# Token routing in a fused scan, gated-MLP and expert kernel: one-hots in bf16, running sums by matmul, gate factors after the counts, addresses read when wanted

## The chip, the cores and the metric

The kernel runs on one core of a Trainium2 chip. The metric is the device time in microseconds of one execution. Five engines appear in the rows: PE (TensorE; PEld is its weight load), DVE (VectorE), ACT (ScalarE), POOL (GpSimd) and SP (SyncE, which here only issues DMAs). Most DMAs are issued from SP's queue, the indirect ones from POOL's.

## What is computed

Cut to what matters here, the reference is three layers in a row over 3072 tokens of 384 features:

```python
x = attn(q, k, v, alpha)                    # gated linear recurrence, 4 x 8 heads
x = moe(x, w_gate, w_val, w_out, rms_g)     # RMS norm, silu(x Wg) * (x Wv), then W_out
logits = x @ r_gate                         # 8 experts
e_idx = argmax(logits, 1)
probs = softmax(logits)
gate = probs[arange(N), e_idx]
eom = sigmoid(x @ r_ogate)
for e in range(8):
    rows = e_idx == e
    out[rows] = gate[rows, None] * eom[rows, e, None] * (relu(x[rows] @ w1[e]) @ w2[e])
```

The routing of the last layer is what the change touches: which expert each token goes to, the token's gate factor, and its place in that expert's list.

## The kernel before, in words

The tokens go through the first two layers in eight groups of 384 (`NG` groups of `GT` = 3 tiles of 128). After a group's last matmul of the second layer, `m_evac` (L689) copies its three tiles out of PSUM into a tile R of 400 columns: 384 features, 8 logits, 8 output-gate logits.

`route_a` (L709) then works on 128 x 3 x 8 numbers at a time, nearly all on DVE: the maximum, the differences, a one-hot of the maximum as float32 (ties broken by `rev8`), a bf16 copy of it (`ohb`), running sums of the three tiles' one-hots in bf16 (`ohc`), the exponentials by way of tanh on ACT, their sum (`se`) and the output gate (`og`). `route_b` (L744) counts with matmuls into a PSUM tile `ps_r` (L748 to L752): a strictly triangular matrix gives a token's rank in its tile, an all-ones matrix on `ohc` adds the tiles in front. DVE makes the gate factor (L755 to L757), the rank (L760 to L763), the row number `pos` (L766) and the new counts `cnt` (L767). Three indirect DMAs from POOL's queue (L769) scatter the rows of R into a `bucket` in DRAM, one region per expert. Groups 0 to 6 are routed while the next group's matmuls run; the last group's routing has no next group behind it.

The experts follow, in order of size. Expert slot 0 is split into two units u = 0 and u = 1 of 256 rows; then one unit per slot. The first unit's rows, weights and first matmuls are prepared from the counts of the first seven groups, so they do not wait for the last group. A unit runs through eight blocks j: `e_h(u, j)` (L1175) is nine matmuls (L650) into `ps_h`, with an eviction by ACT (L1184) and DVE (L1185); `e_o(u, j)` (L1189) is six matmuls (L1211, or L1205 for the slots that are computed transposed). `pop_o` issues `e_o` some blocks behind `e_h`.

Around the last group the program reads: e_h(0,0), the last MLP matmuls, `m_evac`, `route_a(7)` (L1337), e_h(0,1), then in the loop e_h(0,2), e_o(0,0), `route_b(7)` (L1509), `pick_rest` (L1042; it ranks the experts by count and writes the address table `adr`, L1056), the loads of slot 1's weights (L1083, L1098), the rows of unit 1 (L1130, which reads the bucket and so waits for the last scatter), more weights, and the rows of unit 2 (L1136). `addresses(p)` (L1023) reads a slot's three addresses (row region, w1 row, w2 row) from `adr` into SP registers, all three at once (L1025), before the first DMA that uses one. Slot 1's weights are split into a high and a low part by ACT and DVE (L1090, L1091, L1109, L1110) during unit 1.

What sets the order: a scheduler lays out each engine's queue at build time from its own estimate of readiness. `keep_in_program_order` (also called `pin` and, when `strict[0]` is set, `seq`) ties an instruction behind the one written just before it on its engine; everything else may be moved. In the last group `strict` is off until `route_b(7)`, so the scheduler may put e_o(0,1) and e_o(0,2) in front of `ps_r` on PE.

Of the kernel before, what the change touches and what calls it, by code (L numbers as in the profile page):

```python
# [55 lines left out]
def gla_glu_moe_kernel(  # L56
# [120 lines left out]
    def f(x):  # L177
        return x.bitcast(F32)
# [530 lines left out]
    def route_a(g):  # L709
        R = rows[g]  # L710
        L, O = R[:, :, DM:DM + E], R[:, :, DM + E:WO]
        bc = [P, GT, E]
        mx = small("mx", [P, GT, 1])
        nc.vector.tensor_reduce(out=mx, in_=L, op=ALU.max, axis=AX.X)
        ex = small("ex", bc)
        nc.vector.tensor_tensor(out=ex, in0=L, in1=mx.to_broadcast(bc), op=ALU.subtract)
        oh = small("oh", bc)
        nc.vector.tensor_scalar(out=oh, in0=ex, scalar1=0.0, scalar2=None, op0=ALU.is_ge)

        nc.scalar.activation(ex, ex, AF.Tanh, scale=0.5)  # L720
        er_ = small("er_", bc)
        nc.vector.tensor_scalar(out=er_, in0=ex, scalar1=-1.0, scalar2=1.0, op0=ALU.mult, op1=ALU.add)
        nc.vector.reciprocal(out=er_, in_=er_)
        nc.vector.scalar_tensor_tensor(out=ex, in0=ex, scalar=1.0, in1=er_, op0=ALU.add, op1=ALU.mult)
        nc.vector.tensor_tensor(out=oh, in0=oh, in1=rev8.to_broadcast(bc), op=ALU.mult)
        m8 = small("m8", [P, GT, 1])
        nc.vector.tensor_reduce(out=m8, in_=oh, op=ALU.max, axis=AX.X)
        nc.vector.tensor_tensor(out=oh, in0=oh, in1=m8.to_broadcast(bc), op=ALU.is_equal)
        ohb = small("ohb", [P, GT, E], BF16)
        nc.vector.tensor_copy(ohb, oh)  # L730
        ohc = small("ohc", [P, GT, E], BF16)
        nc.vector.tensor_copy(ohc[:, 0, :], oh[:, 0, :])
        nc.vector.tensor_tensor(out=ohc[:, 1, :], in0=oh[:, 0, :], in1=oh[:, 1, :], op=ALU.add)
        nc.vector.tensor_tensor(out=ohc[:, 2, :], in0=ohc[:, 1, :], in1=oh[:, 2, :], op=ALU.add)
        sg = small("sg", bc)
        nc.vector.tensor_tensor(out=sg, in0=oh, in1=O, op=ALU.mult)
        og = small("og", [P, GT, 1])
        nc.vector.tensor_reduce(out=og, in_=sg, op=ALU.add, axis=AX.X)
        nc.scalar.activation(og, og, AF.Tanh, scale=0.5)
        se = small("se", [P, GT, 1])  # L740
        nc.vector.tensor_reduce(out=se, in_=ex, op=ALU.add, axis=AX.X)
        rt[g] = (oh, ohb, ohc, m8, og, se)

    def route_b(g):  # L744
        oh, ohb, ohc, m8, og, se = rt.pop(g)
        R = rows[g]
        ps = psR[0].tile([P, GT + 1, E], F32, tag=psR[1], name="ps_r")
        seq(nc.tensor.matmul(ps[:, 0:1, :], lhsT=tri_b, rhs=ohb[:, 0:1, :], start=True, stop=True))  # L748
        for i in range(1, GT):
            seq(nc.tensor.matmul(ps[:, i, :], lhsT=tri_b, rhs=ohb[:, i, :], start=True, stop=False))  # L750
            seq(nc.tensor.matmul(ps[:, i, :], lhsT=ones_b, rhs=ohc[:, i - 1, :], start=False, stop=True))
        seq(nc.tensor.matmul(ps[:, GT, :], lhsT=ones_b, rhs=ohc[:, GT - 1, :], start=True, stop=True))  # L752
        bc = [P, GT, E]

        nc.vector.tensor_scalar(out=se, in0=se, scalar1=1e-9, scalar2=2.0, op0=ALU.add, op1=ALU.mult)  # L755
        nc.vector.reciprocal(out=se, in_=se)
        nc.vector.scalar_tensor_tensor(out=R[:, :, DM:DM + 1], in0=og, scalar=1.0, in1=se, op0=ALU.add, op1=ALU.mult)  # L757
        nc.vector.tensor_copy(R[:, :, DM + 1:DM + 2], tokid[:, g * GT:g * GT + GT, :])
        rk = small("rk", bc)
        nc.vector.tensor_tensor(out=rk, in0=ps[:, 0:GT, :], in1=cnt.to_broadcast(bc), op=ALU.add)  # L760
        nc.vector.tensor_tensor(out=rk, in0=rk, in1=oh, op=ALU.mult)
        pf = small("pf", [P, GT, 1])
        nc.vector.tensor_reduce(out=pf, in_=rk, op=ALU.add, axis=AX.X)  # L763
        nc.vector.tensor_scalar(out=m8, in0=m8, scalar1=-float(REG), scalar2=float(E * REG), op0=ALU.mult, op1=ALU.add)
        pos = small("pos", [P, GT, 1], I32)
        nc.vector.tensor_tensor(out=pos, in0=pf, in1=m8, op=ALU.add)  # L766
        nc.vector.tensor_tensor(out=cnt[:, 0, :], in0=cnt[:, 0, :], in1=ps[:, GT, :], op=ALU.add)  # L767
        for i in range(GT):
            nc.gpsimd.indirect_dma_start(out=bucket_of[g * GT + i], out_offset=OFF(ap=pos[:, i, 0:1], axis=0),  # L769
                                         in_=R[:, i, 0:RW], in_offset=None)  # L770
# [247 lines left out]
    places = {}  # L1018
# [60 lines left out]
    def load_w1(p, i):  # L1079
        n = F2 // 4  # L1080
        s = slice(i * n, i * n + n)
        st = staging("st1", [P, KD, n])
        ins = nc.sync.dma_start(st, w1.rearrange("e k n -> (e k) n")[bass.ds(places[p][1], DM), s]  # L1083
                                .rearrange("(p kc) n -> p kc n" if p else "(kc p) n -> p kc n", p=P))
        if p > 1:
            pin(ins)

        def go():
            w1h, w1l = we[p][0:2]
            for ins in (nc.scalar.activation(w1h[:, :, s], st, AF.Copy),  # L1090
                        nc.vector.tensor_tensor(out=w1l[:, :, s], in0=st, in1=f(w1h[:, :, s]), op=ALU.subtract)):  # L1091
# [33 lines left out]
    def load_rows(u, er):  # L1125
        p, s0, r, n = parts[u]
        rows_ = bucket[bass.ds(places[p][0], CMAX), :]
        ix = act.tile([P, 4, 1], I32, tag="ix", name="ix", bufs=4)
        if u < 2:
            nc.sync.dma_start(er[:, 0:n, :], rows_[s0:s0 + P * n, :].rearrange("(p b) w -> p b w", b=n))  # L1130
            erow[u] = (er, ix, er[:, :, DM:DM + 1], er[:, :, RW - 1:RW])
            return
# [42 lines left out]
    def e_h(u, j):  # L1175
# [4 lines left out]
        else:  # L1180
# [3 lines left out]
        nc.scalar.activation(hh[:, 0, :], ps, AF.Relu)  # L1184
        nc.vector.scalar_tensor_tensor(out=hh[:, 1, :], in0=ps, scalar=0.0, in1=f(hh[:, 0, :]),  # L1185
                                       op0=ALU.max, op1=ALU.subtract)
        h2[u, j] = hh

    def e_o(u, j, tiles=None):  # L1189
# [18 lines left out]
        for i in range(n) if tiles is None else tiles:  # L1208
            sl = slice(i * r, i * r + r)
            for m, (a_, b_) in enumerate(((0, 2), (0, 3), (1, 2))):  # L1210
                ins = nc.tensor.matmul(ob2[u][i][0:r], lhsT=hh[:, a_, sl], rhs=we[p][b_][:, j, :],  # L1211
                                       start=(j == 0 and m == 0), stop=(j == KF2 - 1 and m == 2))
                if tiles is not None:
                    tc.keep_in_program_order(ins)
# [264 lines left out]
    def pop_o():  # L1479
        u, j = lag.pop(0)  # L1480
        e_o(u, j)
# [11 lines left out]
    for u in range(U):  # L1493
        for j in range(KF2):
# [4 lines left out]
            e_h(u, j)  # L1499
# [95 lines left out]
```

## Time and profile before

| | |
|---|---|
| median of 3 runs | 820.66 us (820.44 to 821.23) |
| the profiled execution | 820.86 us |
| its span, first to last instruction | 819.0 us |
| mean granted TensorE clock | 0.997 |
| PE / DVE / ACT / POOL busy | 98% / 69% / 40% / 11% of the span |
| DMA moved | 106.85 MB, mean 130 GB/s |

A row of the timeline gives start and length in us, the engine, the line of the kernel, the operation, the tile written and the tiles read, and, in square brackets, the idle time of that engine just before it with what ended it. A row of the waits gives who waited for whom, the total, the number of times and the longest, all in us.

### The profile page before, as it was taken

The page shows a single profiled execution, that of the slowest core. Times are in us where ns is not written, and L with a number is a line of the kernel's source. Part 1 is how long each engine was busy: PE and PEld are TensorE (multiplying, and loading weights), DVE is VectorE, ACT ScalarE, POOL GpSimd, SP SyncE. Part 2 cuts the span into 40 slices and gives each one's busy share as a digit, 9 for nine tenths or more (in the row PEclk, how much of TensorE's full clock was granted, in tenths as well). Part 3 has the DMA queues.
Part 4 walks back from the last instruction along what each step waited for, and adds up shares of the span by engine and source line. Part 5 has one row for each costly group of instructions (what it writes and reads, how often), then busy time and mean ns, then how long its engine had stood idle before and what let it go on. Part 6 is the DMA issues. An engine that isn't in the chain of part 4 may idle for free.

```text
span 819.0 us, 15897 instructions
## 1 busy us (share of the span) xinstructions
PE 802.6 (98%) x5967; PEld 771.7 (94%) x5967; DVE 561.4 (69%) x1234; ACT 326.5 (40%) x694; POOL 91.3 (11%) x175
## 2 busy tenths in 40 slices
PE   7999999999999999999999999999999999999996
PEld 5899999999999999999999999999988999999996
DVE  7998999498677876767767662345358667677641
ACT  1756554333333333332433332225226455554441
POOL 3001000000300020010020011010021002211121
PEclk9999999999999999999999999999999999999998
DMA  9955575753543453344444221005047686688710
GB/s 200 215 142 153 160 163 167 214 142 95 146 111 92 113 130 76 83 112 96 102 115 102 47 46 44 20 21 183 1 142 209 169 223 186 214 245 251 204 54 28
DMA packets 195454, 106.85 MB, mean 130 GB/s; under 512 B 125868, under 2 KB 190122, under 8 KB 195376
## 3 DMA queue, kind: packets, MB, share of 16 engines
q1 hardware_dynamic: 190912, 96.35, 46.2%
q0 software_dynamic: 4464, 9.48, 3.5%
q8 instruction: 47, 0.77, 0.4%
q14 instruction: 31, 0.25, 0.1%
HBM read 80.88 MB, written 25.18 MB: 129 GB/s over the span
## 4 chain that ended last, share of the span: by engine, by line
PE 93%; issue 2%; DVE 2%; POOL 1%; ACT 1%; DMA 0%; POOLq 0%; DVEq 0%
PE ps_o L684 19%; PE ps_v L650 19%; PE ps_g L650 19%; PE ps_h L650 12%; PE ps_b L1205 8%; PE ps_s L430 3%; PE ps_b L1211 3%; PE ps_y L468 3%; PE ps_y L464 2%; PE ps_st L489 1%; PE pc L615 1%; PE ps_k L450 1%; PE ps_n L283 1%; DMA er<-bucket 0%; PE pt L607 0%
## 5 line engine op out<-in xcount | busy, mean ns | idle before, releaser
L664 ACT ACTIVATE hh<-tt 128x384 fp32r<-128x384 f32 x96 | 50.3, 524 | 143.2 <-DVE tt L661 133.2
L661 DVE TENSOR_TENSOR tt<-tt,ps_v 128x384 f32<-128x384 f32 x96 | 52.7, 549 | 77.8 <-PE ps_v L650 65.7
L642 ACT ACTIVATE tt<-ps_g 128x384 f32<-128x384 f32 x96 | 47.0, 490 | 86.1 <-PE ps_g L650 80.3
L670 DVE TENSOR_TENSOR hl<-tt,hh 128x384 fp32r<-128x384 f32 x96 | 52.9, 551 | 24.6 <-ACT hh L664 23.0
L1185 DVE SCALAR_TENSOR_TENSOR h<-ps_h,h 128x256 fp32r<-128x256 f32 (+6 forms) x72 | 38.1, 531 | 45.2 <-ACT h L1184 42.5
L684 PE MATMUL ps_o<-wol,hh 128*128 128x400 f32 x192 | 66.3, 346 | 0.0
L684 PE MATMUL ps_o<-woh,hh 128*128 128x400 f32 x192 | 65.2, 348 | 0.0
L1184 ACT ACTIVATE h<-ps_h 128x256 fp32r<-128x256 f32 (+6 forms) x72 | 33.5, 468 | 77.4 <-PE ps_h L650 76.5
L684 PE MATMUL ps_o<-woh,hl 128*128 128x400 f32 x192 | 63.7, 344 | 0.0
L650 PE MATMUL ps_h<-x,w1b 128*128 128x456 f32 (+3 forms) x288 | 57.2, 341 | 0.3 <-DVE h L1185 0.3
L650 PEld LDWEIGHTS ps_h<-x,w1b 128*128 128x128 f32 x288 | 50.6, 188 | 1.9 <-DVE h L1185 0.6
L650 PE MATMUL ps_h<-x,w1a 128*128 128x256 f32 (+3 forms) x288 | 52.2, 325 | 0.0
L650 PEld LDWEIGHTS ps_h<-x,w1a 128*128 128x128 f32 x288 | 47.3, 188 | 0.9 <-ACT x L1165 0.3
L650 PE MATMUL ps_g<-xh,wgh 128*128 128x384 f32 x192 | 46.1, 348 | 0.0
L440 DVE TENSOR_TENSOR P<-ps_s,mask 128x512 f32<-128x512 f32 x46 | 30.1, 685 | 23.0 <-PE ps_s L430 22.8
L650 PE MATMUL ps_v<-xh,wvh 128*128 128x384 f32 x192 | 45.8, 346 | 0.0
L650 PE MATMUL ps_v<-xl,wvh 128*128 128x384 f32 x192 | 44.1, 337 | 0.0
L1205 PE MATMUL ps_b<-h,w2b 128*128 128x456 f32 (+2 forms) x216 | 43.5, 343 | 0.5 <-issue 0.5
L650 PE MATMUL ps_g<-xh,wgl 128*128 128x384 f32 x192 | 44.0, 336 | 0.0
L650 PE MATMUL ps_g<-xl,wgh 128*128 128x384 f32 x192 | 43.8, 337 | 0.0
L650 PE MATMUL ps_v<-xh,wvl 128*128 128x384 f32 x192 | 43.8, 336 | 0.0
L1205 PEld LDWEIGHTS ps_b<-h,w2b 128*128 128x128 f32 x216 | 37.9, 188 | 2.2 <-issue 0.9
(312 smaller groups left out, 1880.3 us busy)
## 6 DMA issues: line engine op xcount, KB each, us to landing
st<-in_moe_w_dram SPq DMA_DIRECT2D x46, 384.0 KB
bucket<-zero SPq DMA_DIRECT2D x8, 772.0 KB
stg<-in_moe_w_gate_dram SPq DMA_DIRECT2D x12, 384.0 KB
stg<-in_moe_w_val_dram SPq DMA_DIRECT2D x12, 384.0 KB
stg<-in_moe_w_out_dram SPq DMA_DIRECT2D x12, 384.0 KB
v<-in_v_dram SPq DMA_DIRECT2D x23, 192.0 KB
more<-in_moe_w_dram SPq DMA_DIRECT2D x9, 384.0 KB
er<-in_moe_w_dram SPq DMA_DIRECT2D x9, 384.0 KB
```

Of the source, the lines that this page charges most:

```text
L430: seq(nc.tensor.matmul(ps[hh][:, p, :], lhsT=kT[r, p, :], rhs=qT[r, p, :], start=True, stop=True))
L440: pace(f'Ph{t}', nc.vector.tensor_tensor(out=Ph, in0=ps[hh], in1=mb, op=ALU.mult))
L468: seq(nc.tensor.matmul(ps[u, h * D:h * D + D], lhsT=Pt[h % 2][:, h // 2, u], rhs=vt[t][:, h, :], start=first, stop=True, skip_group_check= ...
L642: nc.scalar.activation(tt, ps, AF.Silu)
L650: seq(nc.tensor.matmul(ps, lhsT=a_[:, kc, :], rhs=b_[:, kc, :], start=(n == 0), stop=(n == 3 * KD - 1)))
L661: nc.vector.tensor_tensor(out=tt, in0=tt, in1=ps, op=ALU.mult)
L664: nc.scalar.activation(hh, tt, AF.Copy)
L670: nc.vector.tensor_tensor(out=hl, in0=tt, in1=f(hh), op=ALU.subtract)
L684: seq(nc.tensor.matmul(obank[s][i], lhsT=a_[:, sl], rhs=weight(b_, j), start=(j == j0 and n == 0), stop=(j == j1 - 1 and n == 2)))
L1184: nc.scalar.activation(hh[:, 0, :], ps, AF.Relu)
L1185: nc.vector.scalar_tensor_tensor(out=hh[:, 1, :], in0=ps, scalar=0.0, in1=f(hh[:, 0, :]), op0=ALU.max, op1=ALU.subtract)
L1205: nc.tensor.matmul(ob2[u][k_][:, 0:r * n], lhsT=we[p][b_][:, j, k_ * P:k_ * P + P], rhs=hh[:, a_, :], start=(j == 0 and m == 0), stop=(j = ...
```

## The change

The routing of a group becomes one function that hands out eight steps, so that the last group's steps can be put in another order than the other groups'. The float32 one-hot, its bf16 copy and the three instructions of `ohc` become one comparison that writes bf16; the comparison with zero and the product with `rev8` become one instruction. The sums over the tiles in front are made by matmuls of the all-ones matrix with each tile's one-hot: nine matmuls a group in place of six. In the last group the product `sg`, the scaling of `m8` and the copy of the token numbers go to POOL, the DVE steps are pinned in the written order, and the gate factor comes after `pos`. The eviction of e_h(0,2) is written after `route_b(7)` with its DVE half pinned there, and e_o(0,1) is pinned where it is written, behind e_h(0,3). Addresses are read one at a time, when the first DMA that wants one is written; the DMAs of slot 1's weights and of unit 1's rows are now pinned.

```diff
-    def route_a(g):
+    def routing(g):
         R = rows[g]
+        end = g == NG - 1
         L, O = R[:, :, DM:DM + E], R[:, :, DM + E:WO]
...
+        side_ = nc.gpsimd if end else nc.vector
+        def order(ins):
+            if end:
+                tc.keep_in_program_order(ins)
+        def pick():
...
+            nc.vector.tensor_reduce(out=mx, in_=L, op=ALU.max, axis=AX.X)
+            order(nc.vector.tensor_tensor(out=ex, in0=L, in1=mx.to_broadcast(bc), op=ALU.subtract))
+            order(nc.vector.scalar_tensor_tensor(out=oh, in0=ex, scalar=0.0, in1=rev8.to_broadcast(bc),
+                                                 op0=ALU.is_ge, op1=ALU.mult))
+            nc.scalar.activation(ex, ex, AF.Tanh, scale=0.5)
+            order(nc.vector.tensor_reduce(out=m8, in_=oh, op=ALU.max, axis=AX.X))
+            order(nc.vector.tensor_tensor(out=ohb, in0=oh, in1=m8.to_broadcast(bc), op=ALU.is_equal))
+            ins = side_.tensor_tensor(out=sg, in0=ohb, in1=O, op=ALU.mult)
+            if not end:
+                order(ins)
+                order(nc.vector.tensor_reduce(out=og, in_=sg, op=ALU.add, axis=AX.X))
+                nc.scalar.activation(og, og, AF.Tanh, scale=0.5)
+            ins = side_.tensor_scalar(out=m8, in0=m8, scalar1=-float(REG), scalar2=float(E * REG),
+                                      op0=ALU.mult, op1=ALU.add)
...
+        def weigh():
+            order(nc.vector.tensor_scalar(out=er_, in0=ex, scalar1=-1.0, scalar2=1.0, op0=ALU.mult, op1=ALU.add))
+            order(nc.vector.reciprocal(er_, er_))
+            order(nc.vector.scalar_tensor_tensor(out=ex, in0=ex, scalar=1.0, in1=er_, op0=ALU.add, op1=ALU.mult))
+            order(nc.vector.tensor_reduce(out=se, in_=ex, op=ALU.add, axis=AX.X))
+            if end:
+                order(nc.vector.tensor_reduce(out=og, in_=sg, op=ALU.add, axis=AX.X))
+                nc.scalar.activation(og, og, AF.Tanh, scale=0.5)
+            order(nc.vector.tensor_scalar(out=se, in0=se, scalar1=1e-9, scalar2=2.0, op0=ALU.add, op1=ALU.mult))
+            order(nc.vector.reciprocal(se, se))
+        def factor():
+            order(nc.vector.scalar_tensor_tensor(out=R[:, :, DM:DM + 1], in0=og, scalar=1.0, in1=se,
+                                                 op0=ALU.add, op1=ALU.mult))
+            ins = side_.tensor_copy(R[:, :, DM + 1:DM + 2], tokid[:, g * GT:g * GT + GT, :])
...
+        def count():
+            ps = psR[0].tile([P, GT + 1, E], F32, tag=psR[1], name="ps_r")
+            for i in range(GT + 1):
+                terms = [(ones_b, k_) for k_ in range(i)] + ([(tri_b, i)] if i < GT else [])
+                for n, (m_, k_) in enumerate(terms):
+                    seq(nc.tensor.matmul(ps[:, i, :], lhsT=m_, rhs=ohb[:, k_, :],
+                                         start=(n == 0), stop=(n == len(terms) - 1)))
...
     def route_b(g):
+        pick, weigh, factor, count, rank, tally, place, send = rt.pop(g)
+        count()
+        for step in (weigh, rank, place, factor, tally, send) if g == NG - 1 else (factor, rank, place, tally, send):
+            step()
...
+    def place_in(p, i):
+        if i not in places[p]:
+            places[p][i] = wanted[p](i)
+        return places[p][i]
...
     def addresses(p):
-        places[p] = [nc.values_load(adr[0:1, p, i:i + 1], engines=SP, min_val=0, max_val=top[i]) for i in range(3)]
+        places[p] = {}
+        wanted[p] = lambda i: nc.values_load(adr[0:1, p, i:i + 1], engines=SP, min_val=0, max_val=top[i])
...
-        if p > 1:
+        if p:
             pin(ins)
...
         h2[u, j] = hh
+        def evict():
+            nc.scalar.activation(hh[:, 0, :], ps, AF.Relu)
+            ins = nc.vector.scalar_tensor_tensor(out=hh[:, 1, :], in0=ps, scalar=0.0, in1=f(hh[:, 0, :]),
+                                                 op0=ALU.max, op1=ALU.subtract)
+            if (u, j) == (0, 2):
+                pin(ins)
+        if (u, j) != (0, 2):
+            evict()
+        return evict
...
-        e_o(u, j)
+        e_o(u, j, None, (u, j) == (0, 1))
...
                 route_b(NG - 1)
+                evict()
                 pick_rest()
```

## Rows read from the trace of the kernel before

**Rows 1.** Windows: stretch, its length, busy us of each engine, PEclk, DMA share, GB/s.

```profile
31.00:590.00 559.00, 559.00 (x4450) 540.21 (x4447) 393.23 (x893) 213.14 (x497) 46.95 (x92) 1.00 0.43 110
...
607.00:609.00 2.00, 2.00 (x15) 2.00 (x14) 0.42 (x1) 0.39 (x1) 0.00 (x0) 1.00 1.00 338
...
620.00:629.00 9.00, 8.64 (x59) 8.00 (x58) 7.85 (x14) 6.57 (x10) 0.00 (x0) 1.00 0.56 178
...
635.00:806.00 171.00, 171.00 (x961) 167.49 (x961) 112.22 (x195) 81.88 (x132) 25.34 (x21) 1.00 0.65 185
```

**Rows 2.** Waits of PE over the whole span.

```profile
PE ps_t L1161 <- DMA er<-bucket: 1.5, 1, 1.5
...
PE ps_b L1205 <- issue: 0.5, 1, 0.5
...
PE ps_h L650 <- DVE h L1185: 0.3, 1, 0.3
PE ps_b L1211 <- ACT h L1184: 0.2, 1, 0.2
```

**Rows 3.** Timeline of PE, 595 to 612 us.

```profile
595.21 1.23 PE L650 MATMUL ps_h<-x2a,w1a 128*128 128x256 f32 x9
596.28 2.64 PE L1211 MATMUL ps_b<-w2a,h 128*128 128x384 f32 x14
598.76 0.18 PE L748 MATMUL ps_r<-ohb,tri_b 128*128 128x8 bf16 x1
...
598.93 2.39 PE L650 MATMUL ps_h<-x2a,w1a 128*128 128x256 f32 x18
...
602.94 1.23 PE L1211 MATMUL ps_b<-w2a,h 128*128 128x384 f32 x6
604.01 1.24 PE L650 MATMUL ps_h<-x2a,w1a 128*128 128x256 f32 x9
...
611.32 0.85 PE L1161 MATMUL ps_t<-ident,er 128*128 128x128 f32 x6 [1.46 <-DMA er<-bucket]
```

**Rows 4.** Timeline of DVE, 595 to 602 us.

```profile
595.28 0.18 DVE L714 TENSOR_REDUCE mx<-R 128x3 f32<-128x24 f32 x1 [0.17 <-ACT R L700]
...
596.35 0.18 DVE L728 TENSOR_TENSOR oh<-oh,m 128x24 f32<-128x24 f32 x1
...
596.90 0.43 DVE L1185 SCALAR_TENSOR_TENSOR h<-ps_h,h 128x256 fp32r<-128x256 f32 x1
...
599.12 0.18 DVE L760 TENSOR_TENSOR rk<-ps_r,cnt 128x24 f32<-128x24 f32 x1 [0.47 <-PE ps_r L752]
...
599.81 0.16 DVE L766 TENSOR_TENSOR pos<-pf,m 128x3 int32<-128x3 f32 x1
...
602.17 0.17 DVE L1056 TENSOR_TENSOR adr<-kadr,who 128x21 int32<-128x21 f32 x1
```

**Rows 5.** Timeline of POOL and SP, 600 to 608 us.

```profile
600.75 0.96 POOL L769 DMA_INDIRECT bucket<-R,pos  x1 [48.18 <-ACT h L1184]
...
605.11 0.68 SPq L1083 DMA_DIRECT2D st<-in_moe_w_dram  x1
...
607.14 0.34 SPq L1130 DMA_DIRECT2D er<-bucket  x1
```

**Rows 6.** Line 1025, 602 to 605.2 us, then 606 to 632: duration ns min/median/max, first and last start.

```profile
L1025 SPq TENSOR_LOAD <-adr x3: 352/381/462, 602.4 to 603.7; - x3
...
L1025 SPq TENSOR_LOAD <-adr x18: 260/266/292, 615.4 to 629.9; - x18
```

**Rows 7.** Timeline around two of POOL's small instructions, at 182 and at 486 us.

```profile
182.26 0.19 POOL L475 TENSOR_SCALAR ss<-ss 128x1 f32<-128x1 f32 x1 [7.44 <-ACT xn L474]
182.53 0.55 POOL L476 TENSOR_TENSOR ss<-ss,mhalf 128x1 f32<-128x1 f32 x1
...
486.46 0.75 POOL L475 TENSOR_SCALAR ss<-ss 128x1 f32<-128x1 f32 x1 [21.38 <-ACT xn L474]
486.48 0.68 DVE L411 TENSOR_TENSOR qT<-qT,aT 128x512 f32<-128x512 f32 x1
```

More of the change, by code (lines that the diff above doesn't have):

```diff
@@ L744, in route_b @@
-    def route_b(g):
[L745 to L770, printed above, removed]
@@ new lines, in routing @@
+        side_ = nc.gpsimd if end else nc.vector
+        got = {}
+        def order(ins):
+            if end:
+                tc.keep_in_program_order(ins)
+        def pick():
+            for nm in ("mx", "m8", "og", "se"):
+                got[nm] = small(nm, [P, GT, 1])
+            for nm in ("ex", "oh", "sg", "er_", "rk"):
+                got[nm] = small(nm, bc)
+            ohb = got["ohb"] = small("ohb", [P, GT, E], BF16)
+            mx, ex, oh, m8, sg, og = (got[nm] for nm in ("mx", "ex", "oh", "m8", "sg", "og"))
+            nc.vector.tensor_reduce(out=mx, in_=L, op=ALU.max, axis=AX.X)
[12 more added lines that the diff above has]
+                                      op0=ALU.mult, op1=ALU.add)
+            if not end:
+                order(ins)
@@ new lines, in rank, with tally, place @@
+        def rank():
+            ps, rk = got["ps"], got["rk"]
+            order(nc.vector.tensor_tensor(out=rk, in0=ps[:, 0:GT, :], in1=cnt.to_broadcast(bc), op=ALU.add))
+        def tally():
+            order(nc.vector.tensor_tensor(out=cnt[:, 0, :], in0=cnt[:, 0, :], in1=got["ps"][:, GT, :], op=ALU.add))
+        def place():
+            rk, ohb, m8 = got["rk"], got["ohb"], got["m8"]
+            order(nc.vector.tensor_tensor(out=rk, in0=rk, in1=ohb, op=ALU.mult))
+            pf = small("pf", [P, GT, 1])
+            order(nc.vector.tensor_reduce(out=pf, in_=rk, op=ALU.add, axis=AX.X))
+            pos = got["pos"] = small("pos", [P, GT, 1], I32)
+            order(nc.vector.tensor_tensor(out=pos, in0=pf, in1=m8, op=ALU.add))
@@ new lines, in send, with route_a @@
+        def send():
+            for i in range(GT):
+                nc.gpsimd.indirect_dma_start(out=bucket_of[g * GT + i], out_offset=OFF(ap=got["pos"][:, i, 0:1], axis=0),
+                                             in_=R[:, i, 0:RW], in_offset=None)
+        return pick, weigh, factor, count, rank, tally, place, send
+    def route_a(g):
+        rt[g] = routing(g)
+        rt[g][0]()
+        if g < NG - 1:
+            rt[g][1]()
+    def route_b(g):
+        pick, weigh, factor, count, rank, tally, place, send = rt.pop(g)
+        count()
+        for step in (weigh, rank, place, factor, tally, send) if g == NG - 1 else (factor, rank, place, tally, send):
+            step()
@@ L1183, in e_h, with e_o @@
         hh = act.tile([P, 2, r * n], F32R, tag="xl" if j % 2 else "xh", name="h2")
-        nc.scalar.activation(hh[:, 0, :], ps, AF.Relu)
-        nc.vector.scalar_tensor_tensor(out=hh[:, 1, :], in0=ps, scalar=0.0, in1=f(hh[:, 0, :]),
-                                       op0=ALU.max, op1=ALU.subtract)
         h2[u, j] = hh
-    def e_o(u, j, tiles=None):
+        def evict():
[7 more added lines that the diff above has]
+        return evict
+    def e_o(u, j, tiles=None, held=False):
         p, _, r, n = parts[u]
@@ L1212, in e_o @@
                                        start=(j == 0 and m == 0), stop=(j == KF2 - 1 and m == 2))
-                if tiles is not None:
+                if tiles is not None or held:
                     tc.keep_in_program_order(ins)
@@ L1498, in gla_glu_moe_kernel @@
                 pop_o()
-            e_h(u, j)
+            evict = e_h(u, j)
             lag.append((u, j))
```

47 lines of the change are left out of this document (12 added, 35 removed).

## The prediction, on record before the change ran

> **What bounds the kernel now.** I read the page first, then windows, then PE's waits, then the timelines around the last group's routing. PE is busy 98% of the span and without a gap from 31 to 590 us and from 635 to 806 us [rows 1]. So a DVE instruction saved in groups 0 to 6 is worth nothing by itself, and a matmul added there costs its full length. What PE loses in the stretch that the change rewrites stands in its waits [rows 2]: 1.5 us before the transposes of unit 1's rows, which come out of the bucket by DMA, then 0.2, 0.3 and 0.5 us in and behind unit 1, together 2.5 us. Nothing that the change does can give back more than these. A measurement of this kernel can tell a difference of about 0.2%, or 1.64 us, from no change.
>
> **The path to the 1.5 us wait.** The last group's routing starts on DVE at 595.28 and writes the one-hot at 596.35; PE counts at 598.76, filling the time before with e_o blocks; `pos` ends at 599.97 [rows 3, 4]. POOL starts the first scatter at 600.75 [rows 5], 0.78 after `pos`. The rows of unit 1 are asked for at 607.14 [rows 5], behind two weight loads on SP's queue; PE goes on at 611.32 [rows 3], 4.2 us later, while the DMA engines are full, a share of 1.00 from 607 to 609 [rows 1]. The address table is ready at 602.34 [rows 4], yet the first weight load goes out only at 605.11 [rows 5]: three register reads stand between, starting 0.65 us apart [rows 6].
>
> **The change part by part.**
>
> 1. Three more matmuls per group. Six take from 598.76 to 598.93 [rows 3], 0.028 us each. Eight groups: 24 x 0.028 = **+0.68 us**, on PE's path everywhere, with no cover.
>
> 2. Fewer DVE steps (five a group). In groups 0 to 6 PE's lack of gaps hides all of it: 0. In the last group the path to the one-hot loses one dependent step, about 0.2 us (the steps from `rk` to `pos`, three of them, take 0.69 [rows 4]), and the bf16 copy and `ohc` behind it. The one-hot that PE needs then ends at about 596.15 + 0.18 = 596.33.
>
> 3. PE's order. e_o(0,1) and e_o(0,2) may no longer run ahead of the count. e_h(0,2) runs from 595.21 for 1.07 us, and two matmuls of e_o(0,0) are left, 0.18 each [rows 3]: PE comes to the count at 596.63, 0.3 after the one-hot. No wait there, and the count starts 2.1 us sooner. If the one-hot were later, PE would idle by as much, since its filling is gone.
>
> 4. The held eviction. Behind the count PE has e_h(0,3) and e_o(0,1), 1.07 each [rows 3], so until 596.63 + 0.25 + 2.14 = 599.02; then every block needs e_h(0,2) evicted. On DVE the order after the one-hot is seven steps of weights, `rk`, the product, the sum, `pos`, the factor, `cnt`, and then that eviction. With 0.2 for a dependent step, 0.1 for an independent one and 0.3 for the reciprocal of 24 I get `rk` at 597.5, `pos` 598.15, factor 598.25, `cnt` 598.35, eviction from 598.45, 0.43 long [rows 4]: done at 598.9. That is 0.1 in hand, so 0. Every tenth later than that is a tenth of PE idle.
>
> 5. POOL's three small steps. `sg` (two inputs), the scaling of `m8` and the token copy leave DVE. POOL's own small steps last 0.19 with one input and 0.55 with two, and 0.75 where a DVE product of two SBUF tiles runs beside a step [rows 7]. I take 0.55 for `sg`, the row with two inputs: from 596.4 to 596.95, before DVE asks for it at about 597.1. Bounds: 0.19, and 0.75 with a start as late behind its input as the scatter's 0.78 [rows 4, 5], which ends it at 597.9. The scaling ends within 0.75 behind it, by 597.7, before `pos`; the token copy is over by 598.5, before the scatter starts. All three: 0.
> POOL's 0.19 us step is stretched to 0.75 beside DVE's 0.68 us product and ends 0.05 us after it [rows 7]. The Trainium skill (SBUF — State Buffer, section "SBUF: two separate sides") has the rule for this: a DVE instruction with two SBUF inputs and a GpSimd instruction that reads SBUF lock one shared port pair, and whoever comes second waits for the whole instruction of the first. The trace agrees, and the rule speaks against moving `sg` to POOL: by it DVE's next product would wait for `sg` as well, which would put up to 0.55 on the chain of part 4 and make the sum 0.45 longer; by the rows alone it is 0.
>
> 6. The scatter and the read of unit 1's rows. The factor ends at about 598.4; with POOL's 0.78 the first scatter starts at 599.2, 1.55 sooner. The read of unit 1's rows waits for the last scatter and so goes out at 605.6. The weight loads in front: `cnt` is ready 1.1 us sooner, DVE's ranking holds one 0.43 us eviction more, so the addresses come at about 601.5; one register read instead of three in front of the first load saves 1.3 more, and that load goes out near 603.0 instead of 605.11. The second comes behind the first's 0.68 [rows 5] and its own read of 0.65, near 604.3. Both are largely moved before the rows are read, so these take no longer than the 4.2 us of now: PE could go on at 609.8 at the latest. PE wants them at 609.86 + 0.68 / 8, about 609.95. The 1.46 us wait goes: **-1.46**. Bounds: 0 (the transfer is as slow as DMA engines that are full can make it) and the whole.
>
> 7. Register reads spread out. Of 21 reads for slots 1 to 7, 18 stand between 615.4 and 630 [rows 6], in front of or between weight loads of slots 1 and 2. Moved to their DMAs they cost SP the same 0.6 each, at places where PE has no gap, from 635 on [rows 1]: 0. In 615 to 630 the loads come sooner, but DVE is busy 7.85 of 9 us there [rows 1], and PE's 0.3 us wait is for a DVE eviction [rows 2], not for a load. So I leave the three later waits as they are: 0, bounds 0 and -1.06.
>
> Sum: 820.86 + 0.68 - 1.46 = 820.08 for the profiled execution. That execution stands 0.20 above the median of 820.66, so the median becomes **819.9**.
>
> **The rivals.**
>
> *1. As above*, 819.9: chance 0.50.
>
> *2. The later waits go too.* Unit 1 starts 1.4 us sooner and SP is free to bring slot 1's last weights, so DVE's conversions, which crowd 620 to 629, spread out. For it: 18 register reads, some 10 us of SP's time, leave this stretch. Against it: the wait is on DVE, whose work stays. 819.9 - 1.06 = 818.8: chance 0.21, faster.
>
> *3. PE starves on the held eviction.* `og` on DVE waits for POOL's `sg`, and everything pinned behind it, the eviction among it, is late. It decides as soon as DVE reaches the eviction after 598.55. At the upper bounds of part 5 `sg` ends at 597.9 instead of 596.95, DVE stands from 597.1 to 597.9, and PE idles 0.8 less the 0.1 in hand: 820.6. For it: POOL's step that takes 0.75 beside DVE's [rows 7]. Against it: DVE's steps here are 0.2 to 0.4 long, not 0.68. Chance 0.07, within 0.2%. The port rule of part 5 is the same mechanism and would bring it about with a `sg` of 0.55.
>
> *4. The read of unit 1's rows stays late.* The scatter's rows land as late as now, or the weights in front keep the DMA engines full. For it: DMA share 1.00 from 607 to 609 [rows 1]. 819.9 + 1.46 = 821.3: chance 0.15, within 0.2%.
>
> *5. Slower: SP reads registers in the wrong place.* A read is not pinned; only the DMA behind it is. The scheduler lets reads run as soon as the table is there, as it did with 18 of them in a row and between loads [rows 6]. If several land in front of the read of unit 1's rows, each costs 0.65. Part 6 leaves about 0.1 in hand, so n reads cost PE 0.65 n - 0.1; from four on that is 2.5 and more: 822.4, over 0.2% slower, and eight give 825.0. Against it: a read is now written only right before its DMA, most of them long after unit 1's rows, and before the change none stood there. Chance 0.07, slower.
>
> **How the numbers follow.** The likeliest case gives 819.9. Rivals 1, 3 and 4 lie between 819.0 and 822.3; a little of case 1 may reach past 819.0, and rival 2 does. Faster by over 0.2%: 0.21 + 0.06 = 0.27. Slower: 0.07 + 0.01 = 0.08. Between: 0.65. The range takes in rival 2 with 0.3 for the spread of runs below it and rival 4 with 0.1 above: 818.5 to 821.4. Left out are rival 5 and the ends of the others.
>
> **What the profile would show.** Right: nine matmuls of `ps_r` in 0.25 us in each group, the last at about 596.6; no e_o(0,1) in front of them; the first scatter near 599.2; one register read in front of the first weight load, out before 603.5; the read of unit 1's rows near 605.6; no wait of PE before the transposes; PE's waits in 615 to 635 as before. Wrong: a wait of PE before e_h(0,4) or e_o(0,2) near 599 (rival 3, and part 4's sum), a row of PE waiting for the bucket still over 1 us (rival 4), register reads in front of line 1130's successor (rival 5), or no wait left at all up to 635 us (rival 2).

## The result, and the profile after

| | before | after |
|---|---|---|
| median | 820.66 us (820.18 to 821.23, 5 runs) | **827.92 us** (825.96 to 830.43, 5 runs) |
| ratio | | 1.0083 (95% interval 1.0068 to 1.0099) |
| the profiled execution, its span | 820.86, 819.0 us | 827.23, 825.5 us |
| mean granted TensorE clock | 0.997 | 0.998 |
| PE busy | 802.6 us, x5967 | 809.3 us, x5991 |

The change made the kernel slower by 0.8%. Of all matmuls only the 24 that the prediction counted are new, yet PE is busy 6.7 us longer: the first thing to see is that most of the loss is not a wait that the profile lists. The second comes from the windows of the kernel after, those of [rows 1] that lie clear of the routing:

```profile
31.00:590.00 559.00, 559.00 (x4447) 540.23 (x4448) 391.84 (x856) 212.51 (x495) 46.67 (x92) 1.00 0.44 110
...
635.00:806.00 171.00, 169.90 (x940) 163.80 (x940) 112.80 (x198) 81.75 (x132) 27.99 (x23) 1.00 0.67 190
```

From 31 to 590 us PE is as free of gaps as before, at the same clock of 1.00. From 635 to 806 it was free of them and now is not: 1.10 us are missing, and 21 matmuls fewer fit in. PE's waits after, those that answer to [rows 2]:

```profile
PE ps_t L1207 <- DMA er<-bucket: 1.4, 1, 1.4
...
PE ps_b L1258 <- ACT h L1233: 0.5, 1, 0.5
PE ps_h L650 <- ACT x L1211: 0.4, 1, 0.4
...
PE ps_h L650 <- DVE h L1234: 0.3, 1, 0.3
```

The wait that was to go is still 1.4 us; one of 0.4 is new. To see where the time goes, take the start of the same block of matmuls in both timelines. First PE's of the kernel after, then two rows that [rows 3] don't have of the kernel before:

```profile
599.45 1.23 PE L650 MATMUL ps_h<-x2a,w1a 128*128 128x256 f32 x9
...
600.87 0.18 PE L774 MATMUL ps_r<-ohb,tri_b 128*128 128x8 bf16 x1
...
601.11 1.33 PE L650 MATMUL ps_h<-x2a,w1a 128*128 128x256 f32 x9
602.27 1.92 PE L1264 MATMUL ps_b<-w2a,h 128*128 128x384 f32 x10
604.03 1.23 PE L650 MATMUL ps_h<-x2a,w1a 128*128 128x256 f32 x9
...
614.44 0.85 PE L1207 MATMUL ps_t<-ident,er 128*128 128x128 f32 x6 [1.38 <-DMA er<-bucket]
615.04 1.29 PE L1264 MATMUL ps_b<-w2a,h 128*128 128x384 f32 x6
...
638.54 1.51 PE L1258 MATMUL ps_b<-h,w2b 128*128 128x456 f32 x6 [0.49 <-ACT h L1233]
...
808.00 3.29 PE L650 MATMUL ps_h<-x,w1b 128*128 128x384 f32 x18
```

```profile
634.80 1.52 PE L1205 MATMUL ps_b<-h,w2b 128*128 128x456 f32 x6 [0.49 <-issue]
...
801.68 3.29 PE L650 MATMUL ps_h<-x,w1b 128*128 128x384 f32 x18
```

| block | before | after | late by |
|---|---|---|---|
| e_h(0,2), the last block ahead of the last count | 595.21 [rows 3] | 599.45 | 4.24 |
| the transposes of unit 1's rows | 611.32 [rows 3] | 614.44 | 3.12 |
| the block behind the 0.49 us wait | 634.80 | 638.54 | 3.74 |
| the last 18 matmuls of e_h | 801.68 | 808.00 | 6.32 |

So 4.24 us are lost before the last routing, without one PE gap from 31 to 590 us, and 2.6 in the expert stage. The second row looks better than it is: at the transposes the kernel after still owes six matmuls of e_o(0,7), 1.07 us (615.04), which stand in front of them in the kernel before. From the first row to the third both kernels run the same matmuls, the kernel after three more, in 39.59 us before and 39.09 after: the new order around the routing gives back 0.5 us. The prediction looked at this stretch and at little else.

The first part is in the matmuls' own pace. By lines, PE, 31 to 590 us (count, busy us, mean ns), the low-by-high products of the gate in the kernel after and before:

```profile
L650 PE MATMUL ps_g<-xh,wgl 128*128 128x384 f32 x192 | 44.6, 339 | 0.0
```

```profile
L650 PE MATMUL ps_g<-xh,wgl 128*128 128x384 f32 x192 | 44.0, 336 | 0.0
```

A row's mean is longer than its pace, since a matmul's row overlaps the next one's; from start to start, over all neighbouring gate and value products with the same tiles in this stretch, it is 173.2 ns before and 176.1 after. Line 684's 864 `ps_o` matmuls even became 0.6 ns quicker (182.5 and 181.9). There are 8 groups x 12 blocks x 2 products x 9 = 1728 gate and value matmuls: 1728 x 2.9 = 5.0 us at most, less 864 x 0.6 = 0.5. Of the 4.24 in the table, 0.19 were there when the first of these matmuls started (35.03 before, 35.22 after), the 21 new matmuls of the first seven groups take 21 x 0.027 = 0.57, and 3.5 are left for the pace. Their code is the same. What differs is where their operand lies: the change drops the small tile `ohc`, and with it every tile of the pool `act` that lies below the small ones in SBUF moves up by 64 bytes, `xh` from byte 185792 to 185856. The weights did not move.

### The profile page after: what moved, and what is told of

It reads as the page before. It is cut to its first block, busy times and chain, and to the rows that moved or that the text cites. A ratio compares the mean times of both kernels' runs of the same rounds, so it can differ in the third digit from the quotient of the medians.

```text
span 825.5 us, 15900 instructions
## 1 busy us (share of the span) xinstructions
PE 809.3 (98%) x5991; PEld 776.3 (94%) x5991; DVE 559.5 (68%) x1191; ACT 326.3 (40%) x694; POOL 91.6 (11%) x178
## 4 chain that ended last, share of the span: by engine, by line
PE 83%; DVE 5%; DMA 4%; issue 4%; ACT 2%; SPq 1%; POOL 1%; POOLq 0%; DVEq 0%; ACTq 0%
PE ps_o L684 19%; PE ps_g L650 19%; PE ps_v L650 19%; PE ps_h L650 7%; PE ps_s L430 3%; PE ps_b L1258 3%; PE ps_y L468 3%; PE ps_b L1264 2%; PE ps_y L464 2%; DMA obr<-mid_o 2%; PE ps_st L489 1%; PE pc L615 1%; DMA er<-bucket 1%; DMA er<-in_moe_w_dram 1%; PE ps_n L283 1%
```

## The experiments

e1 to e8 ran on one chip, the first four beside 31 runs of the kernel before (median 822.55 us), the others beside 29 (821.32); e9 ran on another beside 15 (821.97). Runs of one kernel there spread over 1.6 to 5.3 us, so the ratios are compared, each with its interval.

### e1: the changed kernel at the old addresses

```
-ohb = small("ohb", [P, GT, E], BF16)
+ohb = small("ohb", [P, 2 * GT + 1, E], BF16)[:, 0:GT, :]
```

> The changed kernel with one more 64-byte strip reserved beside the bf16 one-hot, so that every large tile lies where it lay before; every engine's instructions and their order are those of the changed kernel. Theory 1 (placement): the matmuls of the gated MLP (line 650) came 176.0 ns apart in place of 173.3 from the first group on, long before any routing, because the tiles moved up by 64 bytes when the tile of the running sums went. Then the pace goes back to about 173.3, 1728 x 2.7 ns = 4.7 us go, and the time is about 821 to 823 (827.9 less 4.7 and less whatever else hung on the place). Theory 2 (the new instructions: more matmuls and more hops between engines disturb the others): nothing here changes them, so 827 to 828 and 176.0 ns.

Measured: 825.15 us, ratio 1.0027 (1.0010 to 1.0043), against 1.0083 for the change. The pace is back at 173.2 ns. The 64 bytes cost 0.0083 - 0.0027 = 0.56%, 4.6 us, where each of the two ratios is uncertain by 0.16% either way. But 0.27%, 2.2 us, are left, more than the 0.6 of the added matmuls.

### e2: the kernel before at the new addresses

```
-ohb = small("ohb", [P, GT, E], BF16)
+ohbc = small("ohb", [P, 2 * GT, E], BF16)
+ohb, ohc = ohbc[:, 0:GT, :], ohbc[:, GT:2 * GT, :]
...
-ohc = small("ohc", [P, GT, E], BF16)
...
-pf = small("pf", [P, GT, 1])
+pf = act.tile([P, GT, 1], F32, tag="mx", name="pf", bufs=1)
```

> The kernel before, with its two bf16 one-hot tiles laid side by side in one and the sum's tile laid where the maximum's was, which gives back 64 bytes: every large tile lies where it lies in the changed kernel, and the routing is still the old one. Theory 1: line 650's matmuls come about 176 ns apart and the time is about 825 to 826 (820.7 + 4.7). Theory 2: 820.7 and 173.3 ns.

Measured: 826.04 us, ratio 1.0053 (1.0035 to 1.0070), pace 176.1 ns. The same price from the other side, 4.4 us, with no change of the routing.

The traces give the price by stage. From the first gate matmul (35.03 us before, 35.22 after, 35.13 in e1, 38.76 in e2) to e_h(0,2) (595.21, 599.45, 595.89, 602.47) pass 560.18, 564.23, 560.76 and 563.71 us. The new place costs 3.5 us there with either routing (after less e1, e2 less before), and the 21 new matmuls 0.6 (e1 less before). That the medians say 4.4 to 4.6 and the traces, one execution each, 3.5 is open; the runs' uncertainty covers it.

### e3: the kernel before, tiles 64 bytes lower

```
-ohb = small("ohb", [P, GT, E], BF16)
+ohb = small("ohb", [P, 2 * GT + 1, E], BF16)[:, 0:GT, :]
```

> The kernel before with 64 bytes more reserved beside the bf16 one-hot: every large tile lies 64 bytes lower than before, so 128 lower than in the changed kernel. Theory 1a (it is the address modulo 128 that counts): as slow as the changed kernel's pace, about 176 ns and 825 to 826. Theory 1b (the old place is one of many good ones and the new one a special bad one): 173.3 ns and 820.7. Theory 2: 820.7.

Measured: 823.61 us, ratio 1.0012 (0.9997 to 1.0027), pace 174.0 ns. So it is not that any move hurts, nor that 128 bytes are the period: 64 bytes down cost 0.8 ns a matmul, 64 up 2.9.

### e4: e1, with unit 1's conversion kept behind an eviction

```
-nc.vector.tensor_copy(ix[0:r, 0:n, :], ids[0:r, 0:n, :])
+(pin if u else id)(nc.vector.tensor_copy(ix[0:r, 0:n, :], ids[0:r, 0:n, :]))
```

> The changed kernel with the tiles at their old places and, besides, the conversion of unit 1's row numbers on DVE pinned behind the eviction of e_h(0,7), which the scheduler had put behind it. In the changed kernel that conversion stood 3.9 us on DVE for unit 1's rows, the eviction behind it came only then, and six matmuls of e_o(0,7), 1.07 us, had to wait with it, so that PE stood 1.4 us though the rows came 1.1 us sooner. If that is where the expected gain went, PE's wait before the transposes falls to about 0.3 us and the time to 1.0 us under the first experiment's, about 820 to 821. If the rows themselves are what PE waits for, the wait stays at 1.4 us.

Measured: 825.64 us, ratio 1.0036 (1.0021 to 1.0051), no gain on e1. In the kernel after, DVE's last eviction of slot 0 stands behind the conversion `ix` in DVE's queue and waits with it for the rows, and six matmuls of e_o(0,7) come behind the transposes. I took the one for the cause of the other. In e4 the eviction is done before the rows come, yet the six matmuls still stand behind the transposes, and PE waits 0.8 us (1.5 in e1): their place is set in the order of PE's own queue. That theory fell.

### e5: three addresses read together again, from slot 2 on

What is left of the loss lies in the expert stage, and there the built orders of the two kernels differ on SP in one thing. Before, the three or four fetches of the former expert's results (`obr`) stand in front of the next expert's first weight load; after the change, with the address read inside that load, the load stands in front of them. The expectations say six times; in the traces it is four, of the five places where `obr` is fetched.

```
 places[p] = {}
 wanted[p] = lambda i: nc.values_load(adr[0:1, p, i:i + 1], ...
+if p > 1:
+    for i in range(3):
+        place_in(p, i)
```

> The changed kernel with its tiles at the old addresses (as e1), and one more thing undone: the three numbers of each of the last six expert slots are read together again, where they were read before; slots 0 and 1 are still read one by one. In the built order of SP this puts the fetch of the rows computed by the expert before (obr) back in front of the first weight load of the next expert; ACT's and DVE's orders differ from e1 in a handful of instructions, PE's in one. Theory A (the weight load that waits for a staging buffer holds back the row fetch behind it, the row fetch holds ACT's queue, and ACT's late eviction stops PE where one expert ends): ACT's waits for obr fall from 12.3 us to about 4.4 as before, PE's waits at 759.6 and 762.9 (1.1 and 0.4) go, and the time falls from 825.15 by 2.6 to 3.4 us, to some 822.2: a ratio of 1.000 to 1.001 to before on this chip. Rival B (the expert stage is longer because it starts with its weights late, from the routing change): the time stays at 825, and the stretch from the last row transpose to the end stays 2.6 to 3.4 us longer than before.

Measured: 820.87 us, ratio 0.9999 (0.9984 to 1.0015), 0.28% or 2.3 us less than e1. From 600 us on, PE's waits are these three; the two that e1 had at 759.6 and 762.9 are gone:

```profile
PE ps_t L1210 <- DMA er<-bucket: 1.0, 1, 1.0
...
PE ps_b L1261 <- ACT h L1236: 0.5, 1, 0.5
...
PE ps_h L650 <- DVE h L1237: 0.3, 1, 0.3
```

ACT's waits for `obr` fell less than I had written, from 12.3 us to 8.2 and not to 4.4. It is enough: what counts is whether the late eviction behind them is later than PE's next need.

### e6: the kernel before, addresses read one by one

```
-places[p] = [nc.values_load(adr[0:1, p, i:i + 1], ...) for i in range(3)]
+if p < 2:
+    places[p] = {i: nc.values_load(adr[0:1, p, i:i + 1], ...) for i in range(3)}
+    return
+places[p] = {}
+wanted[p] = lambda i: nc.values_load(adr[0:1, p, i:i + 1], ...)
...
```

> The kernel before with one thing alone: the three numbers of each of the last six expert slots are read one by one, each at its first use. No routing change, no move of a tile; SP's built order differs only in that the first weight load of the next expert stands in front of the row fetch, six times. Theory A: the expert stage loses 2.6 to 3.4 us: a ratio of 1.003 to 1.004, new PE waits for ACT at the ends of experts, ACT's waits for obr about 12 us instead of 4.4. Rival B: a ratio of 1.000, within 0.15%.

Measured: 823.06 us, ratio 1.0021 (1.0008 to 1.0033): 1.7 us, somewhat under the 2.6 to 3.4 expected, and away from the rival's 1.000. The mechanism is best read here, since nothing else was edited. SP's timeline of the kernel before (start, length, line, what is loaded), then of e6:

```profile
749.12 1.29 SPq L1240 DMA_DIRECT2D obr<-mid_o  x3
750.61 0.55 SPq L1083 DMA_DIRECT2D st<-in_moe_w_dram  x1
```

```profile
754.13 0.55 SPq L1093 DMA_DIRECT2D st<-in_moe_w_dram  x1
754.91 1.36 SPq L1250 DMA_DIRECT2D obr<-mid_o  x3
```

The weight load of 384 KB has moved in front of the row fetch. ACT's timeline of the kernel before, and of e6, with what ACT waited for in brackets:

```profile
753.20 0.62 ACT L1249 ACTIVATE obr<-obr,eg 118x384 f32<-118x384 f32 x1 [0.47 <-DMA obr<-mid_o]
```

```profile
760.33 0.62 ACT L1259 ACTIVATE obr<-obr,eg 118x384 f32<-118x384 f32 x1 [3.68 <-DMA obr<-mid_o]
760.85 0.51 ACT L1175 ACTIVATE x<-xt 128x384 fp32r<-128x384 f32 x1
...
762.00 0.43 ACT L1194 ACTIVATE h<-ps_h 128x336 fp32r<-128x336 f32 x1
```

From the fetch's issue to ACT's use of it pass 753.20 - 749.12 = 4.1 us before and 760.33 - 754.91 = 5.4 in e6, on top of the 0.8 that the issue comes later. ACT stands 3.68 us instead of 0.47, and behind it in its queue are the next rows' split, a weight split and the eviction of `ps_h`, which PE needs. PE's timeline of e6:

```profile
762.48 1.19 PE L1215 MATMUL ps_b<-h,w2b 128*128 128x336 f32 x6 [0.37 <-ACT h L1194]
...
765.04 1.48 PE L650 MATMUL ps_h<-x,w1a 128*128 128x384 f32 x7 [0.41 <-ACT x L1175]
```

The kernel after has SP's two rows in the same order (754.97 the load, 755.76 the fetch), and the same of ACT and of PE:

```profile
760.91 0.62 ACT L1302 ACTIVATE obr<-obr,eg 118x384 f32<-118x384 f32 x1 [3.34 <-DMA obr<-mid_o]
```

```profile
762.41 1.85 PE L1258 MATMUL ps_b<-h,w2b 128*128 128x336 f32 x9
...
765.63 1.51 PE L650 MATMUL ps_h<-x,w1a 128*128 128x384 f32 x7 [0.40 <-ACT x L1211]
```

Note the first of the last two rows: 1.85 us for nine matmuls of which the same nine take 1.55 elsewhere, and no idle time in brackets. PE lost 0.3 us there that the list of waits doesn't have; a stretch's loss is read from its length and count, as in the windows above, not from that list alone.

So the cleanest figure is the length of the expert stage, from the block behind the 0.49 us wait to the last 18 matmuls of e_h. PE's timeline in e5, then in e6:

```profile
634.59 1.52 PE L1261 MATMUL ps_b<-h,w2b 128*128 128x456 f32 x6 [0.49 <-ACT h L1236]
...
801.47 3.29 PE L650 MATMUL ps_h<-x,w1b 128*128 128x384 f32 x18
```

```profile
638.21 1.11 PE L1215 MATMUL ps_b<-h,w2b 128*128 128x456 f32 x4 [0.49 <-ACT h L1194]
...
807.94 3.29 PE L650 MATMUL ps_h<-x,w1b 128*128 128x384 f32 x18
```

| the three addresses | expert stage, us |
|---|---|
| read together | 166.88 (before, e5, e7, e9), 166.85 (e3), 167.01 (e2) |
| read one by one | 169.47 (after), 169.53 (e4), 169.73 (e6), 170.25 (e1) |

SP's order costs 2.6 to 3.4 us of this stage, with either routing and at either place of the tiles (e2 lies at the new one). e6's own trace is of its slowest run, 827.05 us: besides the 2.85 us here it lost 1.4 us before the first gate matmul (36.45 against 35.03) and 2.0 from e_h(0,2) to the block behind the 0.49 us wait, where the clock fell, of which the last section tells. Why the median shows 1.7 and not 2.85 is open.

### e7: e5 with the conversion and an eviction held back

```
-nc.vector.tensor_copy(ix[0:r, 0:n, :], ids[0:r, 0:n, :])
+(pin if u else id)(nc.vector.tensor_copy(ix[0:r, 0:n, :], ids[0:r, 0:n, :]))
...
-if (u, j) == (0, 2):
+if u == 0 and j in (2, 3):
     pin(ins)
```

> e5 with two more things: the conversion of unit 1's token numbers to integers is kept behind the eviction of e_h(0,7) on DVE, and the eviction of e_h(0,3) is kept behind the positions. If all three parts of the loss are now named, what is left is the prediction's own sum: 0.7 us for 24 matmuls against up to 1.5 us of the wait on the rows read, so 820 to 821.5, a ratio of 0.998 to 1.001. If the wait on the rows read does not shrink (it was still 0.8 with the conversion alone kept back, in e4), 1.001.

Measured: 821.56 us, ratio 1.0000 (0.9989 to 1.0010), PE's wait for the rows 1.3 us. Within what was expected, and no gain on e5: the two orders on DVE are not what keeps the wait. The first scatter did come 0.8 us sooner (600.31 - 596.33 = 3.98 us behind e_h(0,2), against 600.71 - 595.94 = 4.77 in e5), but the rows took 4.98 us from the issue of their read to PE (606.52 to 611.50), against 3.97 in e5 (606.60 to 610.57).

### e8: the matmul alone at eight places

```
x = right.tile([P, 4608 + 128], F32R, name="x")
...
def views(o):
    return [x[:, s + 16 * o:s + 16 * o + 3 * N].rearrange("p (k n) -> p k n", k=3) for s in (0, 2304)]
...
for n, (w, v) in enumerate(terms(o, j)):
    keep(nc.tensor.matmul(ps[o], lhsT=w, rhs=v, start=(n == 0), stop=(n == 8)))
```

> No part of the computation is done; zeros are written out. After a warm-up of 144 matmuls, the 128x128 by 128x384 matmul of the gate and value products runs alone, 72 times for each of eight places of its moving operand, 64 bytes apart (ps_a 64 bytes below before's place, ps_b at before's, ps_c at after's, up to ps_h), weights at the addresses of the kernel; then the same again with DVE and ACT reading and writing other tiles of the same side of SBUF beside it. Theory C (the place of the moving operand alone sets the pace): ps_b 173 ns start to start, ps_c 176, ps_a 174 to 175, in both series. Rival D (it is a meeting of TensorE's reads with the other engines' accesses in SBUF, whose places moved along): all eight equal in the first series, unequal in the second. Rival E (neither: what moved is the time at which something else runs): all equal in both.

`x` starts at byte 185728, so the operand of `ps_b` lies at 185792, before's place, and that of `ps_c` at 185856. Measured, the clock at 1.00 throughout. PE's timeline where one place ends and the next begins, 72 matmuls apart, in the first series and in the second:

```profile
54.20 0.68 PE L84 MATMUL ps_b<-x,wh 128*128 128x384 f32 x3
...
66.68 0.68 PE L84 MATMUL ps_c<-x,wh 128*128 128x384 f32 x3
...
79.34 0.70 PE L84 MATMUL ps_d<-x,wh 128*128 128x384 f32 x3
```

```profile
154.94 0.68 PE L88 MATMUL ps_b<-x,wh 128*128 128x384 f32 x3
...
167.41 0.68 PE L88 MATMUL ps_c<-x,wh 128*128 128x384 f32 x3
...
180.07 0.70 PE L88 MATMUL ps_d<-x,wh 128*128 128x384 f32 x3
```

At before's place (66.68 - 54.20) / 72 = 173.3 ns, at after's (79.34 - 66.68) / 72 = 175.9 ns, and in the second series (167.41 - 154.94) / 72 = 173.2 and (180.07 - 167.41) / 72 = 175.9. All eight, start to start in ns, from 64 bytes below before's place upward: 173.3, 173.3, 175.9, 176.8, 173.6, 173.3, 175.9, 176.8. It repeats after 256 bytes. DVE's and ACT's work, meant for the second series, ran beside the first, as their queues did not wait for PE's; the windows of `ps_b` in the first series and of `ps_c` in the second show both cases (PE, PEld, DVE, ACT):

```profile
54.20:66.60 12.40, 12.40 (x73) 12.40 (x73) 11.71 (x21) 11.70 (x23) 0.00 (x0) 1.00 0.00 0
...
167.40:180.00 12.60, 12.60 (x73) 12.60 (x73) 0.00 (x0) 0.00 (x0) 0.00 (x0) 1.00 0.00 0
```

With DVE and ACT busy 94% or idle the pace is the same. Theory C holds, D and E fall: the place of the moving operand sets the pace. 1728 x 2.6 ns = 4.5 us, less the 0.5 that line 684 gains, stand against 4.6 and 4.4 by the medians of e1 and e2 and 3.5 by the traces. Open is why e3's place gave 174.0 ns in the kernel and 173.3 alone. The page "SBUF — State Buffer" of the Trainium skill (section "Operand start alignment") asks that an operand start at a multiple of its element size, and says of this that it is about legality, not speed. Both places meet it, and the pace differs all the same.

### e9: e5 with the sums of seven groups back on DVE

```
+if not end:
+    nc.vector.tensor_tensor(out=ohc[:, 1, :], in0=ohb[:, 0, :], in1=ohb[:, 1, :], op=ALU.add)
+    nc.vector.tensor_tensor(out=ohc[:, 2, :], in0=ohc[:, 1, :], in1=ohb[:, 2, :], op=ALU.add)
...
```

> e5 with the running sums of the first seven groups' one-hots made by DVE again (two adds each, straight from the bf16 one-hots); the last group's stay with TensorE. It is 21 matmuls of 27 ns shorter than e5, and its 14 small DVE steps lie beside TensorE. If the prediction's price of the three more matmuls a group is right, it gains 0.57 us on e5: a ratio of 0.999 to before, which is the size of its uncertainty; if the matmuls were hidden, or the DVE steps are not, it stands where e5 stands, 1.000.

Measured: 821.26 us, ratio 0.9994 (0.9982 to 1.0005). Inconclusive: it points the right way and includes no change. In the traces it comes to e_h(0,2) 0.45 us sooner than e5 (595.49 against 595.94), near the 0.57 of the price. In its profiled execution the wait for the rows was 2.5 us, more than the 0.6 at stake. No version of the change was measurably faster than the kernel before.

## Why the prediction was wrong, step by step

I forecast 819.9 us and no measurable change; it is 827.9, above the range and past every rival. By the ratios: 0.56% from the placement (e1), 0.28% from SP's order (e1 to e5), and for all that the prediction did sum, e5's 0.9999, where it had -0.8 us or 0.9990; e5's interval, 0.9984 to 1.0015, holds both. In e5's trace the first part is 0.73 us longer than before (595.94 against 595.21), the stretch from there to the block behind the 0.49 us wait 0.94 shorter (38.65 against 39.59) and the expert stage equal: -0.2 in all. That stretch is 38.54 in e4, 39.30 in e1, 39.23 in e7 and 40.11 in e9, so what the new routing gives by itself is not settled.

**Part 1 was right.** Nine matmuls of `ps_r` stand between 600.87 and 601.11, 27 ns each, and 21 of the new ones make e1's first part 0.58 us longer (560.76 against 560.18).

**Part 2 failed in what it took the removed tile for.** It counted the instructions that write `ohc` and priced them at nothing, rightly. It did not ask what the tile's 64 bytes hold in place. This is some 4.5 of the 7 us by the medians, and no row of before could show it; but that the tiles below it move by 64 bytes follows from the diff, and could have stood in the prediction as an unknown with both signs.

**Parts 3 and 5 were right, part 4 by luck.** Shifted by the 4.24 us, the count starts at 600.87 - 4.24 = 596.63, as forecast, and PE has no gap up to the transposes. DVE's timeline and POOL's in the kernel after:

```profile
601.75 0.15 DVE L780 TENSOR_TENSOR rk<-ps_r,cnt 128x24 f32<-128x24 f32 x1
...
602.89 0.42 DVE L1234 SCALAR_TENSOR_TENSOR h<-ps_h,h 128x256 fp32r<-128x256 f32 x1 [0.56 <-ACT h L1233]
603.23 0.15 DVE L791 TENSOR_TENSOR pos<-pf,m 128x3 int32<-128x3 f32 x1
...
603.45 0.41 DVE L1234 SCALAR_TENSOR_TENSOR h<-ps_h,h 128x256 fp32r<-128x256 f32 x1
```

```profile
600.64 0.23 POOL L738 TENSOR_TENSOR sg<-ohb,R 128x24 f32<-128x24 bf16 x1 [0.41 <-DVE er__7158 L750]
...
604.23 1.06 POOL L795 DMA_INDIRECT bucket<-R,pos  x1 [3.08 <-issue]
```

`sg` takes 0.23 on POOL, near the lower bound of 0.19, and holds no DVE step up. The 0.55 that the prediction took for it is the row of a power (`ALU.pow`, L476), not of any step with two inputs. `sg` ran beside DVE's reciprocal, which reads one tile and took 0.30 (0.29 in the kernel before), so the port rule of the Trainium skill (SBUF — State Buffer, "SBUF: two separate sides"), which speaks of DVE instructions with two SBUF inputs or in a two-port mode, did not visibly come to bear on it, and these rows neither bear it out nor speak against it. POOL's next step, the scaling of `m8`, did run beside a DVE product of two SBUF tiles (600.96 for 0.20 and 601.02 for 0.18 us), and neither is longer than elsewhere by more than 0.01; no wait shows there. In [rows 7] it is POOL's step that is stretched although it starts 0.02 us before the product, so those rows show that one of the two waits, and not that it is the one that starts second. `rk` comes at 601.75 - 4.24 = 597.5, as worked out. `pos` then is 0.84 late (603.23 - 4.24 = 598.99 against 598.15): the scheduler put the eviction of e_h(0,3), which waits 0.56 us for ACT, in front of it.

Part 4's price of nothing held, but not for its reason. The eviction of e_h(0,2) (603.45) was done at 603.86 - 4.24 = 599.62, not at 598.9, and 0.6 after 599.02, where PE was to need it; by the prediction's own rule PE would have idled those 0.6 us. It did not, because the built order has ten matmuls behind e_h(0,3) (602.27), the six of e_o(0,1) and four of e_o(0,2), 0.71 us, which need only ACT's half of that eviction. So PE came to e_h(0,4) at 604.03 - 4.24 = 599.79, 0.17 after it. That was the scheduler's doing and the prediction's luck.

**Part 6 was half right, and its wait stayed.** SP's timeline after:

```profile
607.10 0.69 SPq L1129 DMA_DIRECT2D st<-in_moe_w_dram  x1
...
610.25 0.35 SPq L1176 DMA_DIRECT2D er<-bucket  x1
```

Less the 4.24, the first scatter came 0.76 us sooner (not 1.55), the weight load at 602.86 (forecast 603.0), the read of unit 1's rows at 606.0 (forecast 605.6) and the rows 1.1 sooner; 4.2 us from the read to PE, as before. Yet PE waits 1.38 instead of 1.46. The step that failed is "PE wants them at 609.86 + 0.68 / 8": it took PE's order up to the transposes as fixed. In the new order e_o(0,7)'s six matmuls, 1.07 us, stand behind the transposes (615.04) and not in front, so PE was there sooner by as much as the rows were, with that work still to do. Of the 0.5 us that the stretch did gain, 0.24 are the wait of PE for ACT's eviction [rows 2], which is gone, and which part 7 had left as it was.

**Part 7 failed: 0 was forecast, the expert stage lost 2.6 us.** It priced a read's 0.6 us on SP and found it harmless "at places where PE has no gap". The reads did not even move there; of line 1071's reads all had started by 633.7 us:

```profile
L1071 SPq TENSOR_LOAD <-adr x21: 263/271/747, 606.3 to 633.7; - x21
```

What moved, without any edit of theirs, were the loads behind those reads, past the row fetches in SP's queue. The step should have listed what else is in that queue from 635 us on and who waits for it: `obr`, ACT's queue behind it, PE behind that. Rival 5 had the right engine and the right kind of mishap, SP's order near a read, but at the wrong place and with a price for the reads themselves.

**No gap is not no cost.** That PE is "without a gap" from 635 to 806 us [rows 1] was used as cover; it means the opposite, that a delay of anything that PE needs has no slack elsewhere to be made up in.

## What to carry to other kernels

A tile that is removed or resized moves its neighbours: list the addresses of both builds before blaming or praising an edit, and hold the places fixed (a padded tile is enough) when the edit itself is to be measured. A change of when a value is read can reorder the transfers that use it; compare the order of each DMA queue in both builds, and look for what now stands behind a big load. Where PE is busy all the time, compare the start of one same block at several points of the run: a slow drift is a pace, a step is a wait.

## What the runs showed of the hardware beyond that

A fp32r matmul of 128x384 runs at 173.3 or at 175.9 to 176.8 ns by where its moving operand starts, in a pattern that repeats after 256 bytes (e8): 1.5 to 2%, at a clock of 1.00, and for the first two of these paces alike with DVE and ACT busy or idle beside it.

The same wait of PE before the transposes can cost more than its length. In e3 it was 1.95 us, and the granted clock then fell to 0.50, TensorE's lower level of 1.2 GHz. PE's timeline and a window in it:

```profile
612.33 0.85 PE L1161 MATMUL ps_t<-ident,er 128*128 128x128 f32 x6 [1.95 <-DMA er<-bucket]
613.21 4.98 PE L650 MATMUL ps_h<-x,w1a 128*128 128x256 f32 x27
```

```profile
613.50:616.50 3.00, 3.00 (x16) 3.00 (x16) 0.78 (x3) 0.21 (x1) 0.67 (x1) 0.50 1.21 277
```

The 27 matmuls take 4.98 us, against 3.45 in the kernel before, behind a wait of 1.46 and at 1.00: 1.5 us more. In e6 it is the same, 4.99 us behind a wait of 1.91. The length of the wait alone does not decide it, since in e9 the clock stayed at 1.00 behind one of 2.5 us:

```profile
613.00:617.00 4.00, 4.00 (x32) 3.79 (x32) 1.68 (x6) 1.33 (x3) 1.99 (x2) 1.00 1.24 243
```

What decides it is open. A step of about that size also stands in the runs that were timed alone: of the 31 of the kernel before beside e1 to e4, the 11 with a mean granted clock of 0.997 or 0.998 have a median of 821.2 us, the other 20, from 0.994 to 0.996, one of 822.9. Whether it is the same fall in each is not shown.
